# The second product by seven products in four chunks instead of two, with all attention ahead of them

## The chip, the cores and the metric

The kernel runs on one core of a Trainium2 chip. The metric is device time in microseconds, from the start of the execution to its end; three runs of the kernel before took 905.02, 905.95 and 906.45 us, the median is 905.95.

## The reference

There are two stages. The first is an attention over q, k, v of shape 8 batches x 8 heads x 576 positions x 64. It adds two outputs: a softmax attention among positions at most three apart, and a softmax attention on means of four positions, repeated four times. The second stage takes the result as x (4608 tokens x 512) through a feed-forward net:

```
h = x @ w_in                     # 512 -> 2048
g = h                  where h >= 1
    (h + 1)^2 / 4      where -1 < h < 1
    0                  where h <= -1
out = g @ w_out                  # 2048 -> 512
```

All is float32.

## The kernel before, in words

**Numbers.** A float32 operand of a big product is held as two parts in TensorE's fp32r type, a high part (a cast, on ACT) and a low part (the rest, a subtraction on DVE or POOL). A product is then three matmuls: high x high, low x high and high x low. Weights are cut into parts once, at the start (`convert`).

**Chunks.** The 4608 tokens go in nine chunks of 512. The hidden layer has 16 rows f of 128, taken in eight pairs j. Chunks 0 and 1 compute both products directly (`mm1`, L1083, and `second`, L1111: per row f and per tile t of 128 tokens three matmuls of 512 columns). From chunk 2 on the first product runs as seven products of half size (Winograd's form of Strassen's scheme, `winograd`, L1298): per pair j seven products of six matmuls, 256 columns each, with sums of weights (`sums_of_weights`, once) and of x (`sums_of_x`, per chunk), and sums of the products on DVE (L1308) and ACT (L1305).

**The second product by seven products.** From chunk `TWICE` = 7 on the second product does the same (`twice`, L1214): for each pair j seven products M1 to M7, each of six matmuls of 256 columns, which add up over j in seven PSUM banks (`SUMS`: 0, 1, 2, 4, 5, 6, 7). It needs the curve in three pieces (L1165 to L1167), sums S1 to S4 of the pieces (L1176), five pairs of parts (L1171, L1172), sums of w_out that `sums_of_second` has stored in DRAM (TA and TB, loaded again for each j), and at the end of a chunk seven sums of the banks (`outputs`, L1238). The last pair j of chunk 8 is done directly.

**Attention.** `attention(n)` handles one pair of heads; 32 pairs, four to a batch, are spread among the chunks, so that batch b is over when the first chunk that needs it begins. A pair takes on PE the scores (L399, L444), the transposes (L628, L653, L654) and the products with v (L706, L729); on DVE reductions, sums and normalizing (L381 to L571, L681, L786, L797); on ACT the exponentials; on POOL a subtraction (L508) and two sums of v over four positions, `half` and `quarter` (L580, L583). It writes x into a ring `xr` of 1024 tokens. Most of its tiles have one slot each (qk, v, vp, vd, sl, sp), and it uses PSUM banks 0 to 2.

**What sets the order.** Every operation is an `Op` of a `Plan` with its engine, a cost, the operations that it needs, and its buffers. Three tables hold the answer of a search that was made elsewhere: `ORDER` (the order of all operations), `OTHER` (which of them run on their second engine) and `PLACES` (the place of each buffer). `Plan.run` walks through `ORDER` with its costs, gives each operation a start, and sorts by it; `Plan.emit` writes out the instructions in that order, so each engine and SP's DMA queue have a fixed order. `emit` also lets an earlier matmul wait for a DMA that a later product needs, where the plan finds one with enough lead. `FILLS` puts filler matmuls (L256) into PE's idle time at the start. `sums_of_second` is created beside pairs `JOBS`, `JOBS` + 2 and so on, and the steps of the second products beside the first products of the next pair j, by the list at L1365 to L1374.

Of the kernel before, what the change touches and what calls it, by code (L numbers as in the profile page):

```python
# [8 lines left out]
F32 = mybir.dt.float32  # L9
# [20 lines left out]
RING = 2 * TOK  # L30
# [25 lines left out]
TWICE = B - 1  # L56
JOBS = 14
# [34 lines left out]
class Plan:  # L92


    LATENCY = 0.10
    PE_LATENCY = 0.25
    DMA_LATENCY = 2.0
    ISSUE = 0.45
    BACKLOG = 6.0
    AHEAD = 0.25  # L100
    LANDED = 1.2
    REACH = 2.5
    TO_PE = 0.04
    LATE = 0.10
    FREE = {"PE": 4.5, "ACT": 3.0, "DVE": 1.0, "POOL": 1.4, "SP": 0.75}
    SWITCH = {(0, 1): 0.09, (1, 0): 0.22, (0, 2): 0.02, (2, 0): 0.17, (1, 2): 0.05, (2, 1): 0.05}

# [21 lines left out]
    def run(self, order, other, places):  # L129

        free = dict(self.FREE)
        avail, busy, users, done = {}, set(), {}, set()
        dma_free = port_free = 0.0
        mode = 0
        last = None

        places = iter(places)

        def pick(b):
            units = b.places[next(places)]  # L140
            assert not any((b.pool, u) in busy for u in units)
            return max(avail.get((b.pool, u), 0.0) for u in units), units

        self.done = []
        for n in order:
            o = self.ops[n]
            e, cost, o.fn, port = o.ways[n in other][:4]
            o.eng = e
            assert n not in done and all(d.n in done for d in o.deps), o.name
            done.add(n)  # L150
            t = given = 0.0
            for d in o.deps:
                x = d.start if d in o.follows else d.end
                if d.eng != e:
                    x += self.PE_LATENCY if d.eng == "PE" else self.TO_PE if e == "PE" else self.LATENCY
                    given = max(given, x)
                t = max(t, x)
            t = max(t, free[e], port_free if port else 0.0, dma_free - self.BACKLOG if e == "SP" else 0.0)
            for b in o.bufs:
                if b.units is None:  # L160
                    x, b.units = pick(b)
                    busy.update((b.pool, u) for u in b.units)
                    x += self.TO_PE if e == "PE" else self.LATENCY
                    given, t = max(given, x), max(t, x)
            o.start = t
            if e == "SP":
                free[e] = t + self.ISSUE
                dma_free = max(dma_free, t + self.DMA_LATENCY) + cost
                o.end = dma_free
            else:  # L170
                if e == "PE":
                    if o.after[0] is last:
                        cost = o.after[1]
                    last = o
                    cost += self.SWITCH.get((mode, o.mode), 0.0)
                    if given > free[e] - self.AHEAD and (mode, o.mode) in ((0, 0), (0, 2)):
                        cost += self.LATE
                    mode = o.mode
                free[e] = t + cost
                o.end = t + cost + o.landing  # L180
                if o.moves:
                    dma_free = max(dma_free, t + self.DMA_LATENCY) + o.moves
                if port:
                    port_free = o.end
            self.done.append(o)
            for b in o.bufs:
                b.end = max(b.end, o.end)
                left = users[id(b)] = users.get(id(b), b.users) - 1
                if not left:
                    for u in b.units:  # L190
                        avail[b.pool, u] = b.end
                        busy.discard((b.pool, u))
        assert len(done) == len(self.ops)
        self.done.sort(key=lambda o: o.start)
        return max(o.end for o in self.done)

    def emit(self, tc, fills):
        at, seen, spare = {}, set(), []
        for i, o in enumerate(self.done):
# [5 lines left out]
            if o.eng == "PE":  # L205
                for d in o.deps:
                    if d.eng != "SP" or d.n in seen:
                        continue
                    seen.add(d.n)
                    for k, (j, ends, ins) in enumerate(spare):  # L210
                        if j > at[d.n][0] and ends > d.end + self.LANDED:
                            tc.add_manual_dep(ins, at[d.n][1].name, mybir.DependencyInfo(mybir.DependencyClass.Sync, mybir.DependencyReason.DATA))
                            del spare[k]
                            break
            made = o.fn()
            if o.eng == "SP":
                at[o.n] = i, made.ins
            elif o.eng == "PE":
                spare = [(i, o.end, x.ins) for x in reversed(made[1:])] if made else [x for x in spare if x[1] > o.end - self.REACH]


@with_exitstack
def attention_then_ffn(ctx: ExitStack, tc, qT, kT, vw, vp, vq, band, fours, w_in, w_out, out):
# [13 lines left out]
    minus = cpool.tile([P, P], F32, name="minus")  # L237
    nc.scalar.mul(minus, ident, -1.0)
# [85 lines left out]
    def attention(n):  # L324
# [155 lines left out]
        less = early and n in PE_MAX(K)  # L480
        if early:
            o_m = op("DVE", 0.815, lambda: nc.vector.tensor_reduce(mlb.tile, sl_n(), axis=AX.X, op=ALU.max),
                     [o_sl], [slp, mlb], kk[2], name=name + "max")
            if less:

                def less_max():
                    for c0, c1 in ((SL0, 512), (512, SL0 + NB * WIN)):
                        w0, w1 = (c0 - SL0) // WIN, (c1 - SL0) // WIN
                        nc.tensor.matmul(
                            sl_view()[:, c0 - SL0 : c1 - SL0],  # L490
                            minus,
                            mlb.tile[:, w0:w1].unsqueeze(2).broadcast_to([P, w1 - w0, WIN]),
                            start=False,
                            stop=True,
                            skip_group_check=True,
                        )

                o_s = op("PE", 1.16, less_max, [o_m], [slp, mlb], kk[2], name=name + "lm")
            else:
                o_s = op("DVE", 0.80, lambda: nc.vector.tensor_tensor(slf(), sl_n(), ml_n(), op=ALU.subtract),  # L500
                         [o_m, None if extra else before.get("x")], [slp, mlb, slb], kk[2], name=name + "sub")
        else:
# [7 lines left out]
        o_e = op("ACT", 0.74, lambda: nc.scalar.activation(slf(), sl_n() if less else slf(), AF.Exp, scale=0.125),  # L510
                 [o_s, None if extra else before.get("x")], [slb] + [slp] * less, kk[3], name=name + "exp")
# [65 lines left out]
        vdb = scratch("vd", [P if shares else KB, NKB, P], "vd")  # L577
# [4 lines left out]
        def quarter():  # L582
            nc.gpsimd.tensor_tensor(vdb.tile, vpb.tile[:, :, 0, :], vpb.tile[:, :, 1, :], op=ALU.add)  # L583
# [5 lines left out]
        def whole():  # L589
            nc.vector.tensor_reduce(vdb.tile, vpb.tile.rearrange("k n f c -> k n c f"), axis=AX.X, op=ALU.add)  # L590

        if by_pe:
# [15 lines left out]
            def vd_out(copy):  # L608
                copy(vdb.tile, vsp.tile[:KB, :, 0:P])
# [111 lines left out]
        def pp_quarters():  # L721

            for tail in range(2):
                for r, h in ((0, 0), (1, 1), (1, 0), (0, 1)):
# [4 lines left out]
                    nc.tensor.matmul(pp_v(r)[hs, cs] if tail else pp_v(r)[hs], vdb.tile[rs, tail, hs], w,  # L729
                                     start=not tail, stop=bool(tail), skip_group_check=True)  # L730

        def pp():
            for kb in range(NKB):
                for h in range(2):
# [3 lines left out]
                        vdb.tile[:, kb, hs],  # L738
# [5 lines left out]
        def pp_up():  # L744
            for kb in range(NKB):
                for i, c0, c1 in ((0, 0, QB), (1, 0, QB // 2), (1, QB // 2, QB), (2, 0, QB)):
                    for h in range(2):
# [3 lines left out]
                            vdb.tile[:, kb, h * D : (h + 1) * D],  # L751
# [647 lines left out]
def PE_MAX(k):  # L1399
    return range(k["pm1"])  # L1400


PLANNED = []
# [4 lines left out]
    pm1=0, pv1=2, pu1=1, o1=-7.22, o2=32.66, dk0=-0.05, tl3=20.0, tl=12.56, ts=10.88, so=60.0, sod=55.13, so2=-10.77,  # L1408
# [311 lines left out]
```

## Time and profile before

| what | value |
|---|---|
| median of three runs | 905.95 us (905.02 to 906.45) |
| profiled execution: first to last instruction | 904.0 us |
| around it (median less span) | 1.95 us |
| chunks 2 to 6, from one's first product to the next one's | 97 to 99 us |
| chunk 7, the same | 83 us |

The profile holds one execution. A row of the windows gives for each engine the time in which it was busy and its instructions in brackets. PE is the matmul engine, PEld its weight loads, which run beside the matmuls. Groups by line give the busy time, the mean of one instruction in ns, and the engine's idle time ahead of them with what ended it. L numbers are lines of the kernel before.

### The profile page before, as it was taken

The page shows a single profiled execution, that of the slowest core. Times are in us where ns is not written, and L with a number is a line of the kernel's source. Part 1 is how long each engine was busy: PE and PEld are TensorE (multiplying, and loading weights), DVE is VectorE, ACT ScalarE, POOL GpSimd, SP SyncE. Part 2 cuts the span into 40 slices and gives each one's busy share as a digit, 9 for nine tenths or more (in the row PEclk, how much of TensorE's full clock was granted, in tenths as well). Part 3 has the DMA queues.
Part 4 walks back from the last instruction along what each step waited for, and adds up shares of the span by engine and source line. Part 5 has one row for each costly group of instructions (what it writes and reads, how often), then busy time and mean ns, then how long its engine had stood idle before and what let it go on. Part 6 is the DMA issues. An engine that isn't in the chain of part 4 may idle for free.

```text
span 904.0 us, 21213 instructions
## 1 busy us (share of the span) xinstructions
PE 895.1 (99%) x8577; PEld 794.2 (88%) x8577; DVE 725.9 (80%) x1329; ACT 547.6 (61%) x1143; POOL 162.3 (18%) x154
## 2 busy tenths in 40 slices
PE   9899999999999999999999999999999999999998
PEld 8678888888898988898889888988898889999997
DVE  6999986888877787888878887888876777678767
ACT  5888865545565555656656556556655576576653
POOL 4544453232202100211211102120021000000000
PEclk9999999999999999999999999999999999999999
DMA  9984343676487657777687667776675468889982
GB/s 330 375 308 158 112 138 120 208 257 225 139 278 271 247 205 258 239 260 249 213 284 251 216 209 258 260 247 218 216 284 199 152 205 286 298 288 302 334 281 90
DMA packets 73226, 214.00 MB, mean 237 GB/s; under 512 B 8088, under 2 KB 11288, under 8 KB 73128
## 3 DMA queue, kind: packets, MB, share of 16 engines
q1 hardware_dynamic: 67864, 204.23, 65.6%
q10 hardware_dynamic: 5264, 8.42, 2.5%
q8 instruction: 67, 1.10, 0.5%
q14 instruction: 31, 0.25, 0.1%
HBM read 180.11 MB, written 32.51 MB: 235 GB/s over the span
## 4 chain that ended last, share of the span: by engine, by line
PE 96%; DVE 2%; ACT 1%; issue 0%; DVEq 0%; POOL 0%; POOLq 0%
PE ps L1111 34%; PE ps L1298 32%; PE ps L1083 9%; PE ps L1214 8%; PE ps L399 3%; PE ps L706 3%; PE ps L628 2%; PE ps L444 1%; PE ps L729 1%; PE ps L653 1%; PE ps L252 0%; DVE xr L1238 0%; PE ps L654 0%; PE ps L599 0%; DVE gt L1065 0%; DVE w_i L849 0%
## 5 line engine op out<-in xcount | busy, mean ns | idle before, releaser
L1111 PE MATMUL ps<-w_o,gt 128*128 128x512 f32 x1368 | 349.8, 395 | 0.6 <-DVE gt L1065 0.6
L1111 PEld LDWEIGHTS ps<-w_o,gt 128*128 128x128 f32 x1368 | 245.2, 188 | 47.4 <-DVE gt L1065 1.3
L1298 PE MATMUL ps<-T,lS 128*128 128x256 f32 x1008 | 147.7, 282 | 0.0
L1298 PEld LDWEIGHTS ps<-T,lS 128*128 128x128 f32 x1008 | 133.4, 188 | 3.9
L1305 ACT COPY tt<-ps 128x512 f32<-128x512 f32 x112 | 65.7, 586 | 94.5 <-PE ps L1298 93.8
L1308 DVE TENSOR_TENSOR tt<-ps,tt 128x512 f32<-128x512 f32 x112 | 62.4, 557 | 58.4 <-PE ps L1298 57.0
L1298 PE MATMUL ps<-B,lA 128*128 128x256 f32 x672 | 101.4, 286 | 0.0
L1298 PEld LDWEIGHTS ps<-B,lA 128*128 128x128 f32 x672 | 91.1, 188 | 7.6 <-ACT tt L1305 0.5
L1083 PE MATMUL ps<-x,w_i 128*128 128x512 f32 x384 | 95.7, 397 | 1.0 <-DVE x L875 0.4
L508 POOL TENSOR_TENSOR sl<-sl,mxl 128x640 f32<-128x640 f32 x29 | 39.9, 1374 | 291.9 <-DVE mxl L506 201.8
L1049 ACT ACTIVATE tt<-tt 128x512 f32<-128x512 f32 x82 | 51.5, 630 | 63.0 <-DVE tt L1308 53.3
L1063 ACT CAST gt<-tt 128x512 fp32r<-128x512 f32 x108 | 66.4, 621 | 37.5 <-PE ps L1111 21.8
L1083 PEld LDWEIGHTS ps<-x,w_i 128*128 128x128 f32 x384 | 70.8, 188 | 18.3 <-DVE x L875 0.9
L1065 DVE TENSOR_TENSOR gt<-tt,gt 128x512 fp32r<-128x512 f32 x96 | 70.3, 739 | 9.2 <-ACT gt L1063 8.6
L1054 ACT ACTIVATE tt<-tt 128x512 f32<-128x512 f32 x113 | 70.6, 630 | 2.3
L1061 DVE SCALAR_TENSOR_TENSOR tt<-tt 128x512 f32<-128x512 f32 x82 | 58.7, 722 | 9.1 <-ACT tt L1054 8.9
L580 POOL TENSOR_TENSOR vp<-vp 128x512 f32<-128x512 f32 (+1 forms) x30 | 41.7, 1391 | 87.4 <-DMA vp<-vq 85.0
L1308 DVE TENSOR_TENSOR tt<-tt 128x512 f32<-128x512 f32 x56 | 40.9, 731 | 13.4 <-ACT tt L1305 12.8
L1298 PE MATMUL ps<-B,lS 128*128 128x256 f32 x336 | 49.7, 284 | 0.0
L1298 PEld LDWEIGHTS ps<-B,lS 128*128 128x128 f32 x336 | 46.1, 189 | 3.4
L1298 PE MATMUL ps<-T,lA 128*128 128x256 f32 x336 | 49.0, 281 | 0.0
L1298 PEld LDWEIGHTS ps<-T,lA 128*128 128x128 f32 x336 | 43.9, 189 | 0.3
(155 smaller groups left out, 1471.9 us busy)
## 6 DMA issues: line engine op xcount, KB each, us to landing
lS<-S SPq DMA_DIRECT2D x112, 512.0 KB, 4.7
lA<-A SPq DMA_DIRECT2D x56, 512.0 KB, 5.0
vp<-vq SPq DMA_DIRECT2D x28, 512.0 KB, 5.1
lA<-A SPq DMA_DIRECT2D x56, 256.0 KB, 3.8
v<-vw SPq DMA_DIRECT2D x32, 320.0 KB, 4.5
raw_i<-w_in SPq DMA_DIRECT2D x16, 512.0 KB, 7.7
raw_o<-w_out SPq DMA_DIRECT2D x16, 512.0 KB, 8.4
qk<-qT SPq DMA_DIRECT2D x28, 288.0 KB, 3.8
```

The costliest lines, as they stand in the source:

```text
L580: nc.gpsimd.tensor_tensor(vpb.tile[:, :, 0:2, :], vpb.tile[:, :, 0:2, :], vpb.tile[:, :, 2:4, :], op=ALU.add)
L1049: o2 = op("ACT", 0.49 + e, lambda: nc.scalar.activation(u(), src(), AF.Relu, bias=0.5, scale=0.5), deps, [srcbuf, ub], key, name=f"relu {n ...
L1054: nc.scalar.activation(u(), u(), AF.Square)
L1061: o4 = op("DVE", v, lambda: nc.vector.scalar_tensor_tensor(g(), src(), 1.0, u(), op0=ALU.max, op1=ALU.min), [o3], [srcbuf, ub], key, name= ...
L1063: o5 = op("ACT", 0.50 + e, lambda: nc.scalar.copy(flat(gb.tile[:, 0]), g()), [o4], [held, gb], key, name=f"gh {name}")
L1065: engine.tensor_tensor(flat(gb.tile[:, 1]), g(), flat(gb.tile[:, 0]), op=ALU.subtract)
L1083: nc.tensor.matmul(hb.tile[:, 0, :], wb.tile[:, w, cc * P : (cc + 1) * P], xt[:, x], start=cc == 0 and i == 0, stop=cc == NCC - 1 and i == 2)
L1111: made = [nc.tensor.matmul(o, gb.tile[:, g, ts], wb.tile[:, w, :], start=i0 + i == 0, stop=i0 + i == 3 * nf - 1) for i, (g, w) in enumerat ...
L1214: made.append(nc.tensor.matmul(o, g.tile[:, gx, ts], w.tile[:, wx, ws], start=j == 0 and h == 0 and i == 0, stop=2 * j + 2 == last_f(c) an ...
L1298: made.append(nc.tensor.matmul(xy(dst), l(w, k), yb.tile[:, v, k], start=first and n == 0, stop=n == 5, skip_group_check=True))
L1305: return op("ACT", cost, lambda: nc.scalar.copy(to(), src()), deps, [tb, XY], kx[i], name=f"{name} {c},{j}")
L1308: return op("DVE", cost, lambda: nc.vector.tensor_tensor(to(), a(), b(), op=ALU.add), deps, held, kx[i], name=f"{name} {c},{j}", port=port)
```

## The change

`TWICE` goes from 7 to 5, so chunks 5 to 8 use the seven products for the second product too. The ring of x grows from two chunks to four, `JOBS` goes from 14 to 8, and a new `ORDER` has all attention over by the time the first of the second products of chunk 5 begins. For pairs from batch 1 on, the pooled v (`vd`) is no longer a tile of its own but the first part of vp's tile. An unused way to subtract the maximum on PE (`PE_MAX`, `less_max`) and its tile `minus` go. `Plan.run` with its costs becomes `Plan.place`, which only looks up places; the order of emission is now `ORDER` itself. Which earlier matmul waits for which DMA comes from a table `CARRIED`. `FILLS` goes from 39 matmuls to 27. The Bass object is made with a DMA scratch of 1024.

```diff
-RING = 2 * TOK
+NRING = 4
+RING = NRING * TOK
...
-TWICE = B - 1
-JOBS = 14
+TWICE = B - 3
+JOBS = 8
...
-    def run(self, order, other, places):
...
+    def place(self, order, other, places):
+
+        busy, users, done = set(), {}, set()
         places = iter(places)
...
+            o.eng, _, o.fn = o.ways[n in other][:3]
             assert n not in done and all(d.n in done for d in o.deps), o.name
             done.add(n)
...
+                    b.units = b.places[next(places)]
+                    units = {(b.pool, u) for u in b.units}
+                    assert not units & busy, o.name
+                    busy |= units
...
-    def emit(self, tc, fills):
...
+    def emit(self, tc, fills, carried):
...
             made = o.fn()
             if o.eng == "SP":
-                at[o.n] = i, made.ins
-            elif o.eng == "PE":
-                spare = [(i, o.end, x.ins) for x in reversed(made[1:])] if made else [x for x in spare if x[1] > o.end - self.REACH]
+                issued[o.n] = made.ins
+            for d, x in zip(carried.get(o.n, ()), reversed(made[1:] if made and o.n in carried else ())):
+                tc.add_manual_dep(x.ins, issued[d].name, mybir.DependencyInfo(mybir.DependencyClass.Sync, mybir.DependencyReason.DATA))
...
-    minus = cpool.tile([P, P], F32, name="minus")
-    nc.scalar.mul(minus, ident, -1.0)
...
-        vdb = scratch("vd", [P if shares else KB, NKB, P], "vd")
+        vdb = vpb if shares else sbuf("vd", [KB, NKB, P], F32, "w", SLOTS)
+
+        def vd():
+            return vpb.tile[:, :, 0, :] if shares else vdb.tile
...
         def quarter():
-            nc.gpsimd.tensor_tensor(vdb.tile, vpb.tile[:, :, 0, :], vpb.tile[:, :, 1, :], op=ALU.add)
+            nc.gpsimd.tensor_tensor(vd(), vpb.tile[:, :, 0, :], vpb.tile[:, :, 1, :], op=ALU.add)
...
-        places = [tuple(range(u, u + n)) for u in range(0, 8, n) if c == NCH or u // 4 == c % 2]
+        places = [tuple(range(u, u + n)) for u in range(0, 4 * NRING, n) if c == NCH or u // 4 == c % NRING]
...
-    total = plan.run(ORDER, OTHER, PLACES)
-    PLANNED.append((total, plan))
+    plan.place(ORDER, OTHER, PLACES)
     with tc.manual_schedule():
-        plan.emit(tc, FILLS)
+        plan.emit(tc, FILLS, CARRIED)
...
-FILLS = {17: (0, 9), 19: (5, 4), 97: (2, 21), 306: (3, 5)}
+CARRIED = {
+    334: (477,), 345: (501, 502), 362: (504,), 372: (528, 529), 385: (531,), 422: (555, 556), 435: (558,), 454: (770,
...
+FILLS = {17: (1, 3), 84: (1, 6), 101: (3, 11), 70: (6, 3), 306: (6, 4)}
...
-    nc = bacc.Bacc("TRN2", target_bir_lowering=False, num_devices=1)
+    nc = bacc.Bacc("TRN2", target_bir_lowering=False, num_devices=1, dynamic_dma_scratch_size=1024)
```

## Rows read from the trace of the kernel before

**Rows 1.** The page, parts 1 and 5: busy us, share, instructions.

```profile
PE 895.1 (99%) x8577; PEld 794.2 (88%) x8577; DVE 725.9 (80%) x1329; ACT 547.6 (61%) x1143; POOL 162.3 (18%) x154
...
L1298 PEld LDWEIGHTS ps<-T,lS 128*128 128x128 f32 x1008 | 133.4, 188 | 3.9
```

**Rows 2.** The page, part 4: the chain that ended last, by engine and line.

```profile
PE 96%; DVE 2%; ACT 1%; issue 0%; DVEq 0%; POOL 0%; POOLq 0%
PE ps L1111 34%; PE ps L1298 32%; PE ps L1083 9%; PE ps L1214 8%; PE ps L399 3%; PE ps L706 3%; PE ps L628 2%; PE ps L444 1%; PE ps L729 1%; PE ps L653 1%; PE ps L252 0%; DVE xr L1238 0%; PE ps L654 0%; PE ps L599 0%; DVE gt L1065 0%; DVE w_i L849 0%
```

**Rows 3.** Waits of PE and of DVE: us in total, times, longest us.

```profile
PE ps L252 <- POOL ident masks.py:199: 1.4, 1, 1.4
...
DVE tt L1308 <- PE ps L1298: 57.0, 81, 2.4
DVE tt L1061 <- ACT tt L1054: 23.3, 23, 5.5
```

**Rows 4.** Chain in time order and timeline: start us, us, instructions.

```profile
61.77 4.14 PE ps L1111 x18
154.12 2.81 PE ps L1111 x12
267.58 2.09 PE ps L1111 x9
...
853.80 0.87 PE L1214 MATMUL ps<-lTA,g 128*128 128x256 f32 x6
854.51 0.87 PE L1214 MATMUL ps<-w_o,g 128*128 128x256 f32 x6
855.22 0.88 PE L1298 MATMUL ps<-B,lA 128*128 128x256 f32 x6
```

**Rows 5.** Windows: length, busy us (instructions) by engine, PEclk, DMA share, GB/s.

```profile
0.00:35.00 35.00, 31.98 (x562) 27.51 (x562) 24.39 (x45) 22.05 (x55) 16.08 (x37) 1.00 0.96 354
35.00:140.00 105.00, 103.43 (x855) 82.59 (x852) 96.06 (x163) 82.67 (x166) 47.85 (x37) 1.00 0.53 188
140.00:728.00 588.00, 587.97 (x5795) 516.25 (x5794) 472.72 (x852) 338.04 (x702) 98.35 (x81) 1.00 0.67 231
728.00:893.00 165.00, 165.00 (x1343) 162.79 (x1342) 125.33 (x260) 103.17 (x219) 0.00 (x0) 1.00 0.81 273
40.00:60.00 20.00, 19.18 (x182) 14.78 (x183) 19.76 (x30) 16.79 (x35) 9.59 (x7) 1.00 0.84 319
60.00:100.00 40.00, 40.00 (x323) 32.41 (x322) 37.48 (x66) 34.82 (x71) 21.74 (x17) 1.00 0.48 165
```

**Rows 6.** DMA issues: count, KB each, median us to landing.

```profile
vp<-vq SPq DMA_DIRECT2D x28, 512.0 KB, 5.1
```

**Rows 7.** DVE by line and shape, 237 to 728 us: busy, mean ns, idle before.

```profile
L1065 DVE TENSOR_TENSOR gt<-tt,gt 128x512 fp32r<-128x512 f32 x79 | 57.0, 730 | 8.0 <-ACT gt L1063 7.5
L1061 DVE SCALAR_TENSOR_TENSOR tt<-tt 128x512 f32<-128x512 f32 x78 | 55.9, 724 | 9.1 <-ACT tt L1054 8.9
L1308 DVE TENSOR_TENSOR tt<-tt 128x512 f32<-128x512 f32 x40 | 29.9, 748 | 9.3 <-ACT tt L1305 8.8
L1308 DVE TENSOR_TENSOR tt<-ps,tt 128x512 f32<-128x512 f32 x40 | 27.6, 690 | 16.3 <-PE ps L1298 15.7
L1308 DVE TENSOR_TENSOR tt<-ps,tt 128x256 f32<-128x256 f32 x40 | 16.9, 423 | 19.1 <-PE ps L1298 18.4
L931 DVE TENSOR_TENSOR T<-tt,T 128x512 fp32r<-128x512 f32 x20 | 13.7, 684 | 0.3 <-ACT T L930 0.3
L931 DVE TENSOR_TENSOR B<-xr,B 128x512 fp32r<-128x512 f32 x15 | 11.5, 771 | 0.0
```

**Rows 8.** A line of DVE beside POOL, two of POOL, whole span.

```profile
L849 DVE TENSOR_TENSOR w_i<-tt,w_i 128x512 fp32r<-128x512 f32 x9 | 9.4, 1049 | 0.7 <-ACT w_i L844 0.7
L580 POOL TENSOR_TENSOR vp<-vp 128x512 f32<-128x512 f32 (+1 forms) x30 | 41.7, 1391 | 87.4 <-DMA vp<-vq 85.0
L583 POOL TENSOR_TENSOR vd<-vp 128x256 f32<-128x256 f32 (+1 forms) x30 | 25.4, 848 | 60.5 <-PE ps L729 59.6
```

More of the change, by code (lines that the diff above doesn't have):

```diff
@@ L92 @@
 class Plan:
[L95 to L106, printed above, removed]
     def __init__(self, warm=0.0, fill=None):
@@ L127, in op @@
         return o
-    def run(self, order, other, places):
[L131 to L135, printed above, removed]
+    def place(self, order, other, places):
+        busy, users, done = set(), {}, set()
         places = iter(places)
[L139 to L142, printed above, removed]
         self.done = []
@@ L146, in run @@
             o = self.ops[n]
-            e, cost, o.fn, port = o.ways[n in other][:4]
-            o.eng = e
+            o.eng, _, o.fn = o.ways[n in other][:3]
             assert n not in done and all(d.n in done for d in o.deps), o.name
             done.add(n)
[L151 to L157, printed above, removed]
@@ L158, in run @@
-            t = max(t, free[e], port_free if port else 0.0, dma_free - self.BACKLOG if e == "SP" else 0.0)
             for b in o.bufs:
                 if b.units is None:
[L161 to L184, printed above, removed]
@@ L185, in run @@
-            self.done.append(o)
+                    b.units = b.places[next(places)]
+                    units = {(b.pool, u) for u in b.units}
+                    assert not units & busy, o.name
+                    busy |= units
             for b in o.bufs:
-                b.end = max(b.end, o.end)
                 left = users[id(b)] = users.get(id(b), b.users) - 1
                 if not left:
-                    for u in b.units:
-                        avail[b.pool, u] = b.end
-                        busy.discard((b.pool, u))
+                    busy -= {(b.pool, u) for u in b.units}
@@ L193, in run @@
+            self.done.append(o)
         assert len(done) == len(self.ops)
-        self.done.sort(key=lambda o: o.start)
-        return max(o.end for o in self.done)
-    def emit(self, tc, fills):
-        at, seen, spare = {}, set(), []
-        for i, o in enumerate(self.done):
+    def emit(self, tc, fills, carried):
+        issued = {}
+        for o in self.done:
             if o.n in fills:
@@ L478, in ml_n @@
             return mlb.tile.unsqueeze(2).broadcast_to([P, NB, WIN])
-        less = early and n in PE_MAX(K)
         if early:
@@ L483, in attention @@
                      [o_sl], [slp, mlb], kk[2], name=name + "max")
[L484 to L501, printed above, removed]
+            o_s = op("DVE", 0.80, lambda: nc.vector.tensor_tensor(slf(), sl_n(), ml_n(), op=ALU.subtract),
+                     [o_m, None if extra else before.get("x")], [slp, mlb, slb], kk[2], name=name + "sub")
         else:
@@ L509, in attention @@
                      [o_m], [slb, mlb], kk[2], name=name + "sub", port=True)
-        o_e = op("ACT", 0.74, lambda: nc.scalar.activation(slf(), sl_n() if less else slf(), AF.Exp, scale=0.125),
-                 [o_s, None if extra else before.get("x")], [slb] + [slp] * less, kk[3], name=name + "exp")
+        o_e = op("ACT", 0.74, lambda: nc.scalar.activation(slf(), slf(), AF.Exp, scale=0.125),
+                 [o_s, None if extra else before.get("x")], [slb], kk[3], name=name + "exp")
         spb = scratch("sp", [P, NQB * SD + P * shares], "sp")
@@ L589, in whole @@
         def whole():
-            nc.vector.tensor_reduce(vdb.tile, vpb.tile.rearrange("k n f c -> k n c f"), axis=AX.X, op=ALU.add)
+            nc.vector.tensor_reduce(vd(), vpb.tile.rearrange("k n f c -> k n c f"), axis=AX.X, op=ALU.add)
         if by_pe:
@@ L608, in vd_out @@
             def vd_out(copy):
-                copy(vdb.tile, vsp.tile[:KB, :, 0:P])
+                copy(vd(), vsp.tile[:KB, :, 0:P])
             o_vs = op("PE", 1.2, fours_of, [l_v, l_fours, None if extra else before.get("x")], [vsp, vb, foursb], kk[4], name=name + "vs", mode=1)
@@ L728, in pp_quarters @@
                     w = apr()[rs, h].rearrange("k x s -> k (x s)")[:, r * QB // 2 : r * QB // 2 + SD // 2] if tail else apm()[rs, :, h, :]
-                    nc.tensor.matmul(pp_v(r)[hs, cs] if tail else pp_v(r)[hs], vdb.tile[rs, tail, hs], w,
+                    nc.tensor.matmul(pp_v(r)[hs, cs] if tail else pp_v(r)[hs], vd()[rs, tail, hs], w,
                                      start=not tail, stop=bool(tail), skip_group_check=True)
@@ L737, in pp @@
                         pp_v()[hs],
-                        vdb.tile[:, kb, hs],
+                        vd()[:, kb, hs],
                         apb.tile[:, kb, :, h, :],
```

18 lines of the change are left out of this document (3 added, 15 removed), and 541 rows, old and new, of tables (CARRIED, ORDER, OTHER, PLACES).

## The prediction, made before the changed kernel was run

> **What bounds the kernel now.** I read the page first: PE is busy 895.1 of 904.0 us, DVE 725.9 (80%) [rows 1], at a granted clock of 1.00 (the 2.4 GHz level) in every window [rows 5]; the chain that ended last is PE for 96%, and its longest lines are the three big products [rows 2]. The longest wait seen from PE is 1.4 us, at the start, while DVE itself waits 57 us for PE's first products [rows 3]. A busy PE could still be a slow one, so I asked for the pace next. In the chain, nine 128x512 matmuls take 2.09 us, twelve 2.80 and eighteen 4.14, so 230 to 234 ns, 232 taken; in the timeline of the last chunk, sets of six 128x256 matmuls begin at 853.80, 854.51 and 855.22, so 0.71 us for six, 118.3 ns each, whether they are the first product (L1298) or the second (L1214) [rows 4]. PE is therefore paced by its columns, back to back, from about 140 us to the last chunk. Last, the windows by stage: between 140 and 728 us PE is idle for 0.03 us, DVE is busy 472.7 of 588 us; between 728 and 893, where the second product already runs as seven products and no attention is left, PE is never idle [rows 5]. So time goes down with PE's columns, as long as DVE, the next engine, keeps up.
>
> The profiled execution has a span of 904.0 us, the median of the runs is 905.95: 1.95 us lie around the span. I take the change of the span and add it to the median.
>
> **The change part by part.**
>
> *Second product of chunks 5 and 6 (TWICE 7 to 5).* Removed: per chunk 16 rows f x 4 tiles x 3 = 192 matmuls of 512 columns at L1111, so 384; added: 8 pairs j x 42 = 336 of 256 columns at L1214, so 672. 384 x 232 ns = 89.1 us go, 672 x 118.3 ns = 79.5 us come: **-9.6 us** on PE. Ends: 384 x 230 - 672 x 119 = -8.4; 384 x 234 - 672 x 118 = -10.6. All of it lies on the path, since PE's work of each chunk follows the last without a gap.
>
> In one sentence by itself: the Trainium skill ("TensorE: Matmul & The Clock Gate", Back-to-back issue gap) gives a sustained spacing of about 131 ns for 512 columns and 81 for 128 when each matmul has its weight load; about 98 for 256 is my estimate between the two, and by it this step would cost 672 x 98 - 384 x 131, some 16 us more. Rows 4 contradict it for this data type: 232 and 118 ns, loads included.
>
> What the seven products add elsewhere: per pair j, DVE trades two 512-wide curves and two 512-wide low parts for three curves, five low parts and four sums. The two stages that have it already show the total: 125.3 us of DVE in 165 us, 76%, with PE full [rows 5]. ACT has 103.2 there, 63%. Hidden beside PE: 0. The extra loads (TA and TB, 512 KB each per j, as large as vp's, which land in 5.1 us [rows 6]) put the DMA share at 0.81 in that window against 0.67 before it; the same comes to chunks 5 and 6, cost 0. That chunks hand over well (T sums written into the earlier chunk's ring, outputs after it) is seen at the boundary 7 to 8, inside the same window.
>
> *All attention ahead.* Banks 0 to 2 and the slots sl, sp, v, vp, qk are needed by the seven products, so pairs 20 to 31 must be over where chunk 5 begins. No work is added, but its place changes: counted through the order table of the diff, the local products of the pairs of batches 2 to 7 stand 16 to 18 us of PE work apart, where they stand 21 to 24 apart now (with 30 and more at a chunk's turn). On PE this costs 0, as each pair takes its time in either place. On DVE it does cost. One feed-forward chunk of the present form takes on DVE, from the rows between 237 and 728 us (five chunks): 57.0 + 55.9 + 29.9 + 27.6 + 16.9 + 13.7 + 11.5, and 20 instructions of L913, of the same kind and size as L931's at 684 ns, 13.7, in all 226 / 5 = 45 us [rows 7]. Such durations overlap by their ends, so 45 is an upper figure; 41 is a lower one (I scale by the window's busy time over the sum of the groups' times, 0.91). Chunks 5 and 6 leave the stretch behind 140 us, and with them 82 to 90 of DVE's 472.7 us and 2 x 84.3 us of PE (per chunk 336 x 0.1183 + 192 x 0.232). What stays is 383 to 391 us of DVE beside 588 - 168.6 = 419 us of PE: **91 to 93%** against 80% now. Can DVE do that? Between 60 and 100 us it is 37.48 of 40 busy, 93.7%, with PE 40.00 full and POOL at 54%; between 40 and 60 it reaches 19.76 of 20, but there PE loses 0.8 us [rows 5]. So the demand sits at, or just under, the best share seen to cost nothing. With a sustained share s the stretch takes max(419, 387/s): no cost for s above 92.4%, 3 us at 91.7%, 11 us at 90%. Ends 0 and +13, taken **+1.0**: the nearest rows are those at 93.7%, but the order in which DVE takes its work is fixed, and somewhere in 400 us it will be late once or twice.
>
> Port: a DVE instruction with two SBUF inputs waits while POOL works; L849, run on DVE beside POOL, takes 1049 ns [rows 8] where L931, the same kind, takes 684 [rows 7]. POOL's work is the same per pair and no longer spread over 490 us but over 400. Some 0.3 us for each collision, and most of these are already in the durations above. Taken within the +1.0.
>
> *vd kept in vp's place.* The loaded tile now lives until the pair's products have read it, so the next pair's 512 KB load starts after them: 5.1 us to land [rows 6] and 1.4 + 0.85 us on POOL [rows 8], 7.4 us of the 16 to 18 us between pairs. Cover 9 us. The load is a wait on SP's queue, and the weight loads lA and lS stand behind it; the load of v, which needs the same products over, stands in that queue already, next to it, so nothing is held longer than now. Cost 0; if the cover goes, rival 3.
>
> *Ring of four chunks, scratch of 1024, no minus tile.* Space and one ACT instruction of 0.3 us at the start: 0. *Sums of the second weights from pair 8 instead of 14*: the same instructions, their DVE time is counted above as all of them lie in the stretch before and after; their stores and POOL neighbours keep their size.
>
> *Start.* Filler matmuls go from 39 to 27, DVE and POOL swap some conversions, and SP's order is new. The first 35 us hold 3.0 us of idle PE and move data at a DMA share of 0.96, and 35 to 140 another 1.6 us [rows 5]. Bytes don't change. Bounds: all of the 4.6 us goes, or as much comes again. Taken 0.
>
> *Carried waits.* Which earlier matmul waits for a DMA is now written in a table instead of found by a rule. A late DMA could cost PE something in either direction, but none of its longest waits is one [rows 3]; taken 0.
>
> Sum: 905.95 - 9.6 + 1.0 = **897.4**.
>
> **The rivals.**
> 1. *DVE becomes the bound (the other side).* Place: between 140 and about 560 us, above all chunks 2 to 4, where the order has a pair every 17 us. Price: 387/s - 419. It decides from a sustained share under 90.1%: then the time is 905.95 or more; at 89% it is 896.4 + 16 = 912. For it: this kernel holds 93.7% only for 40 us, its average is 80%, and the tail of a chain through ACT (L1061 waits on ACT for 23 us in all [rows 3]) needs room. Against: in that stretch DVE now waits mostly for PE (the 57 us of rows 3), that is, it is early, and such slack can be filled. In a milder form, s from 90.5 to 91.5%, the time is 900 to 904.
> 2. *The tables also take out the losses that are there.* The 4.6 us before 140 us go, and the 1.0 us that I took for DVE stays away: 896.4 - 4.6 = 891.8, so 891 to 894. For it: the start has idle PE. Against: its DMA share is 0.96.
> 3. *vp comes late.* If SP's queue holds the load more than 9 us behind other loads, each of 24 pairs makes PE wait 0.5 to 1 us: 897 + 12 to 24. Against: the share of DMA in that stretch is 0.67, and landings take 5 us.
> 4. *Matmuls priced by piece.* If the half-wide ones went at the pace of their loads (188 ns mean [rows 1]), the step would add 672 x 0.188 - 89.1 = 37 us. Rows 4 and 5 show the very same instructions at 118, so hardly any chance. (The skill's spacing, quoted above, is of this kind, and the trace does not bear it out.)
> 5. *It doesn't do what it says*: PE's columns don't fall, 905 to 907. The counts follow from the loops, so 0.01.
>
> **How the numbers follow.** Forecast (894 to 900) 0.62; rival 1 mild (900 to 904.1) 0.10, hard (over 904.1) 0.09; rival 2 0.12; rival 3 0.05; rivals 4 and 5 0.01 each. About 0.2%, 1.8 us, is what a measurement can tell from no change. Faster than 904.1: 0.62 + 0.10 + 0.12 = 0.84, lowered to 0.82 for causes I don't see. Within 0.2% (904.1 to 907.8): 0.01 of rival 5 and some 0.05 of rivals 1 and 3, 0.06. Slower: 0.12. The range 892.5 to 904.0 holds the forecast, the mild rival 1 and most of rival 2.
>
> **What would show it.** Right: 984 matmuls at L1111's successor and 1302 at that of L1214, at 232 and 118 ns; PE idle after 140 us under 2 us; chunk 5's first product at some 559 to 561 us and chunks 5, 6, 7 some 80 to 84 us apart; DVE at 91% or more before it and about 76 to 85% after. Rival 1: PE waits on DVE (sl, gt, xr) between 230 and 560 us, DVE at its own ceiling. Rival 2: PE idle under 2 us in the first 140. Rival 3: PE waits at the pair's products on POOL vp. I am wrong if chunk 5 starts after 568 us, or if the chunks behind it are over 85 us apart.

## The result, and the profile after

The changed kernel took 897.87 us (median of 4 runs, 895.42 to 899.19), the kernel before 905.49 on the same chip: ratio 0.9913, 95% interval 0.9896 to 0.9930. The forecast was 897.4, in a range of 892.5 to 904.0. Run again (run e1_same below) it took 899.71 against 905.97 (medians), ratio 0.9918 (0.9905 to 0.9931). The ratios are taken over all the runs, not from the two medians. The medians differ by 7.6 us where the sum has 8.6. That it came so near is partly luck: two of its terms were wrong by some 4 us each, with opposite signs.

The profiled execution (span 893.5 us) is the quickest of its four. The page's part 1, two lines of its part 4, and the groups of the two second products:

```profile
PE 886.2 (99%) x8853; PEld 798.6 (89%) x8853; DVE 761.6 (85%) x1464; ACT 563.6 (63%) x1217; POOL 162.1 (18%) x153
...
PE 94%; DVE 2%; DMA 2%; ACT 1%; issue 1%; POOL 0%; DVEq 0%; POOLq 0%; ACTq 0%; SPq 0%
...
L1030 PE MATMUL ps<-w_o,gt 128*128 128x512 f32 x984 | 255.5, 398 | 0.1
...
L1133 PE MATMUL ps<-lTA,g 128*128 128x256 f32 x372 | 54.4, 281 | 0.1
```

Against [rows 1] PE has 276 matmuls more (672 - 384 - 12 fillers) and is 8.9 us less busy; against [rows 2] DMA has come into the chain with 2% (landings of vp, of qk and of an output store), where it had no share. PE's and DVE's waits, as in [rows 3] (L1217, L980, L973 were L1298, L1061, L1054):

```profile
PE ps L185 <- POOL ident masks.py:199: 1.4, 1, 1.4
PE ps L625 <- ACT al L581: 0.6, 1, 0.6
```

```profile
DVE tt L1227 <- PE ps L1217: 33.9, 48, 1.6
DVE tt L980 <- ACT tt L973: 10.6, 14, 1.6
```

PE's longest wait is the same 1.4 us, and the others are short, so this execution by itself shows hardly a loss; DVE's slack against PE fell from 57.0 to 33.9 us. The pace, from the chain in order of time (start, us, instructions), is that of [rows 4]: nine matmuls of 512 columns in 2.10 us, six of 256 in 0.71, first product (L1217) and second (L1133) alike:

```profile
299.99 2.10 PE ps L1030 x9
302.08 0.70 PE ps L1217 x6
...
650.59 0.71 PE ps L1217 x6
651.30 0.71 PE ps L1133 x6
```

Windows by stage (columns as in [rows 5]), cut where chunk 0, chunk 1 and chunk 5 begin their first products; then the densest part of the third, and chunk 6 alone:

```profile
0.00:32.10 32.10, 29.75 (x551) 25.54 (x551) 24.80 (x45) 23.15 (x58) 18.61 (x37) 1.00 0.94 329
32.10:134.40 102.30, 102.30 (x893) 81.05 (x892) 91.76 (x158) 81.03 (x163) 41.96 (x36) 1.00 0.62 229
134.40:556.70 422.30, 421.25 (x4639) 363.53 (x4638) 379.75 (x710) 249.42 (x547) 101.57 (x81) 1.00 0.69 242
556.70:893.50 336.80, 332.88 (x2775) 328.54 (x2773) 265.25 (x554) 210.01 (x452) 0.00 (x0) 1.00 0.82 281
...
244.00:456.00 212.00, 211.90 (x2461) 187.16 (x2461) 196.40 (x367) 130.27 (x286) 46.75 (x37) 1.00 0.76 266
...
642.00:722.00 80.00, 80.00 (x675) 79.91 (x675) 65.64 (x138) 53.43 (x115) 0.00 (x0) 1.00 0.89 296
```

Three things are to be seen. The start is 3 us shorter (before, chunk 0 began at 35.1 us). Between 244 and 456 us DVE is 92.6% busy and PE still loses only 0.1 us. And chunk 6 takes 80 us, with 672 matmuls x 0.1183 = 79.5. The landings of vp, as in [rows 6], and of the stores of TA:

```profile
vp<-vq SPq DMA_DIRECT2D x28, 512.0 KB, 4.2
...
TA<-TAs SPq DMA_DIRECT2D x8, 512.0 KB, 3.5
```

### The profile page after: what moved, and what is told of

Read it like the earlier page. It is cut to its first block, busy times and chain, and to the rows that moved or that the text cites. A ratio compares the mean times of both kernels' runs of the same rounds, so it can differ in the third digit from the quotient of the medians.

```text
span 893.5 us, 22025 instructions
## 1 busy us (share of the span) xinstructions
PE 886.2 (99%) x8853; PEld 798.6 (89%) x8853; DVE 761.6 (85%) x1464; ACT 563.6 (63%) x1217; POOL 162.1 (18%) x153
## 4 chain that ended last, share of the span: by engine, by line
PE 94%; DVE 2%; DMA 2%; ACT 1%; issue 1%; POOL 0%; DVEq 0%; POOLq 0%; ACTq 0%; SPq 0%
PE ps L1217 31%; PE ps L1030 24%; PE ps L1133 16%; PE ps L1002 9%; PE ps L332 3%; PE ps L625 3%; PE ps L547 2%; PE ps L377 1%; PE ps L648 1%; PE ps L572 1%; DMA vp<-vq 1%; DMA qk<-qT 1%; DMA out<-tt 0%; PE ps L185 0%; PE ps L573 0%
## 5 line engine op out<-in xcount | busy, mean ns | idle before, releaser
L1030 PE MATMUL ps<-w_o,gt 128*128 128x512 f32 x984 | 255.5, 398 | 0.1
L1030 PEld LDWEIGHTS ps<-w_o,gt 128*128 128x128 f32 x984 | 175.4, 188 | 36.0 <-DVE gt L984 1.1
L1217 PE MATMUL ps<-T,lS 128*128 128x256 f32 x1008 | 147.7, 282 | 0.0
L1217 PEld LDWEIGHTS ps<-T,lS 128*128 128x128 f32 x1008 | 131.9, 189 | 2.1
L1224 ACT COPY tt<-ps 128x512 f32<-128x512 f32 x112 | 65.6, 586 | 59.1 <-PE ps L1217 58.5
L1217 PE MATMUL ps<-B,lA 128*128 128x256 f32 x672 | 101.9, 287 | 0.0
L1217 PEld LDWEIGHTS ps<-B,lA 128*128 128x128 f32 x672 | 88.9, 188 | 5.0 <-DVE tt L1227 0.5
L1227 DVE TENSOR_TENSOR tt<-ps,tt 128x512 f32<-128x512 f32 x112 | 62.2, 555 | 35.0 <-PE ps L1217 33.9
L1084 ACT ACTIVATE tt<-tt 128x256 f32<-128x256 f32 (+1 forms) x93 | 45.4, 489 | 58.2 <-DVE tt L1227 48.1
L457 ACT ACTIVATE sp<-ps,mxp 128x144 f32<-128x144 f32 x96 | 36.6, 381 | 35.9 <-DVE mxp L451 30.2
L1086 DVE SCALAR_TENSOR_TENSOR tt<-tt 128x256 f32<-128x256 f32 (+1 forms) x93 | 46.3, 509 | 10.1 <-ACT tt L1085 10.0
L1133 PE MATMUL ps<-lTA,g 128*128 128x256 f32 x372 | 54.4, 281 | 0.1
L1091 DVE TENSOR_TENSOR g<-s,g 128x256 fp32r<-128x256 f32 (+1 forms) x93 | 46.5, 508 | 8.9 <-ACT g L1090 8.5
L973 ACT ACTIVATE tt<-tt 128x512 f32<-128x512 f32 x80 | 50.6, 632 | 2.2 <-ACT tt L1046 0.4
L1090 ACT CAST g<-s 128x256 fp32r<-128x256 f32 (+1 forms) x93 | 42.6, 473 | 13.5 <-DVE s L1095 13.0
L968 ACT ACTIVATE tt<-tt 128x512 f32<-128x512 f32 x50 | 31.6, 632 | 30.8 <-DVE tt L1227 21.3
L984 DVE TENSOR_TENSOR gt<-tt,gt 128x512 fp32r<-128x512 f32 x64 | 48.6, 762 | 1.7 <-ACT gt L982 1.4
```

The lines of the kernel that those rows point to most:

```text
L973: nc.scalar.activation(u(), u(), AF.Square)
L984: engine.tensor_tensor(flat(gb.tile[:, 1]), g(), flat(gb.tile[:, 0]), op=ALU.subtract)
L1030: made = [nc.tensor.matmul(o, gb.tile[:, g, ts], wb.tile[:, w, :], start=i0 + i == 0, stop=i0 + i == 3 * nf - 1) for i, (g, w) in enumerat ...
L1084: o2 = op("ACT", a, lambda: nc.scalar.activation(u(), src(), AF.Relu, bias=0.5, scale=0.5), deps, [hb, ub], kk[k], name=f"relu {c},{j},{wh ...
L1086: return op("DVE", v, lambda: nc.vector.scalar_tensor_tensor(src(), src(), 1.0, u(), op0=ALU.max, op1=ALU.min), [o3], [hb, ub], kk[k], nam ...
L1091: o2 = op("DVE", v, lambda: nc.vector.tensor_tensor(dst()[:, 1], src(), dst()[:, 0], op=ALU.subtract), [o1], [srcbuf, buf], kk[k], name=f" ...
```

## The experiments

Ratios are to the kernel before, on the same chip, with 95% intervals; two runs are compared by the difference of their ratios, times 906 us. The dense stretch is the one from chunk 1's first product to that of the first chunk that has no pair of attention of its own (chunk 5; in the kernel before and in e6 and e8 chunk 7). Line numbers of a run may be a few higher than the changed kernel's.

**e1_same: the changed kernel again.**

> The changed kernel again, unaltered, for a narrower interval and a second profile. Both theories: 896 to 899 us, ratio to the kernel before 0.990 to 0.993. If DVE is at its limit in the stretch from 134 to 557 us, that stretch differs by 1 to 3 us from the first profile and PE waits on DVE there; if the executions differ by something else, the difference lies at the start or is spread.

0.9918 (0.9905 to 0.9931), 897.11 to 899.97 us. Its profiled execution, 898.0 us, is 4.5 us longer than the first one, and shows what that one lacks. Its windows, the same two stages:

```profile
134.70:560.60 425.90, 421.93 (x4639) 364.07 (x4638) 381.32 (x710) 249.29 (x547) 101.27 (x81) 1.00 0.69 240
560.60:898.00 337.40, 333.44 (x2775) 328.59 (x2773) 265.49 (x554) 209.49 (x452) 0.00 (x0) 1.00 0.80 280
```

PE is idle 4.0 us in the dense stretch against 1.05 in the first profile, with the same work. The longest wait, in the chain of waits:

```profile
265.20 9.69 DMA TA<-TAs
274.92 0.35 ACT TBs L945
...
275.44 0.59 ACT tt L1224
276.08 0.98 PE ps L1217 x6
```

Read it backwards: PE's product waits for a copy out of its bank (L1224), the copy stands on ACT behind a cast (L945), and the cast waits until TA, whose staging tile it writes, has been stored. The store took 9.69 us; a 512 KB store of TA takes 3.5 us in the median of the first profile. PE's next waits in that stretch are 1.0 us on DVE (L980, behind a load of qk that took 5.93 us) and 0.7 us on ACT; the first profile has the wait on DVE too, with 0.5 us.

**e2_undo_both and e11_undo_one: the second product direct again** in chunks 5 and 6 (e2) or 5 alone (e11), with all attention still ahead.

```
-TWICE = B - 3
+TWICE = B - 1        # e11: B - 2
-            if c > TWICE:        # sums of x keep their ring places
+            if c > B - 3:
...                               # ORDER: direct steps in the places of the others
```

> Chunks 5 and 6 get the direct second product back, 384 matmuls of 512 columns in place of 672 of 256; attention, its order, the ring, the tables of the rest stay as in the changed kernel. Theory (the gain is PE's columns, 9.6 us): 897.9 + 9.6 = 907.5, between 906 and 909.5, so 1 to 3 us slower than the kernel before. Rival (the gain came from the new tables or the start): under 902.

> As e2, but chunk 5 alone gets its direct second product back (192 matmuls of 512 columns in place of 336 of 256). Columns: 4.8 us. In e2 another 12 us came from waits at places where the direct form meets an order made for the other one. Theory: 4.8 us and 2 to 7 of such waits, 7 to 12 us slower than the changed kernel, with the difference less the waits at 4.8. Rival (columns are no price there): the difference less the waits at 2 or under.

e2: 1.0152 (1.0129 to 1.0175); e11: 1.0102 (1.0088 to 1.0116). So undoing costs 21 and 17 us beside e1's ratio, not 9.6 and 4.8; both are outside what was expected. Chunks 5 to 7 of e2, of e1 and one stretch of e2, windows:

```profile
564.00:831.00 267.00, 258.67 (x1779) 234.15 (x1777) 146.30 (x269) 142.03 (x268) 0.00 (x0) 0.99 0.60 204
...
680.00:700.00 20.00, 16.72 (x94) 14.48 (x93) 7.39 (x12) 8.04 (x14) 0.00 (x0) 0.91 0.40 142
```

```profile
561.00:806.00 245.00, 244.89 (x2061) 241.90 (x2060) 194.60 (x408) 158.19 (x342) 0.00 (x0) 1.00 0.83 288
```

Of the 22 us, PE's idle time is 8.3 - 0.1 = 8.2; the busy time grew by 13.8, which holds the 9.6 us of columns, some 1.8 us of a lower granted clock (an estimate: the 0.91 over 20 us above) and 2.4 us more that are not explained. In e11, read in the same way, PE is idle 7.8 us and busy 8.3 us longer, where the columns are 4.8. Two waits of e2, us in total, times, longest:

```profile
PE ps L1217 <- ACT tt L1224: 4.7, 3, 3.3
PE ps L1030 <- ACT tt L1046: 1.4, 2, 1.1
```

A direct chunk without attention beside it doesn't run full in this order: DVE is at 55%, and nothing fills PE while a copy (L1224, L1046) is late. So the columns' worth can't be read from the undoing. In this order, which was made for the other form, attention ahead with the old second product is a loss of 1.5%; what an order made for it would give, no run shows.

**e10_pe_more and e7_pe_less: 96 matmuls of 256 columns more, or fewer**, in the second product of chunks 5 and 6 (48 each, 11.4 us in all; e10 repeats the low x high part of M3 to M5, the low part of the curve's factor with the high part of the weights', and e7 leaves it out).

```
-for i, (gx, wx) in enumerate(((0, 0), (0, 1), (1, 0))):
+kinds = ((0, 0), (0, 1), (1, 0))[: 2 if c < 7 and x in ("M3", "M4", "M5") else 3]   # e7
+kinds = ((0, 0), (0, 1), (1, 0)) + ((1, 0),) * (c < 7 and x in ("M3", "M4", "M5"))  # e10
+for i, (gx, wx) in enumerate(kinds):
```

> The changed kernel with the third matmul of M3, M4 and M5 made twice in chunks 5 and 6: 96 matmuls of 256 columns more, 11.4 us at 118.3 ns (the low part of one factor counts twice there). e7 took 96 away and gained 1 to 2 us, as PE then waits on the copies out of the first product's bank. Theory (PE's columns and the loop through that bank are about equally long, so what is added costs in full and what is removed gains nothing): 10 to 12.5 us slower than the changed kernel. Rival (the loop alone sets the pace of chunks 5 and 6): under 5 us slower.

> The changed kernel without one of the three matmuls of M3, M4 and M5 in chunks 5 and 6 (96 of 256 columns left out). Theory (PE's columns bound chunks 5 and 6 at 118.3 ns each): 11.4 us less than the changed kernel, between 10 and 12. Rival (DVE or loads bound these chunks): less than 7 us.

e10: 1.0044 (1.0029 to 1.0059), 0.0126 above e1, 11.4 us, as its theory said: the columns count in full. In its profile chunks 5 to 7 take 88.9, 85.1 and 82.0 us, 10.0 more than e1's 85.5, 80.2 and 80.3, and PE is never idle in chunk 6:

```profile
650.00:735.00 85.00, 85.00 (x722) 85.00 (x721) 65.64 (x138) 53.51 (x115) 0.00 (x0) 1.00 0.82 280
```

e7: 0.9903 (0.9891 to 0.9916), 0.0015 below e1, 1.4 us of 11.4, within the intervals; what was expected of it failed. Chunk 6 of e7, and the waits of PE's weight loads there and in chunk 5, two of e7 and then the only one of e1 on that line:

```profile
645.00:724.00 79.00, 77.65 (x624) 74.61 (x624) 65.48 (x138) 53.01 (x114) 0.00 (x0) 1.00 0.86 298
```

```profile
PEld ps L1218 <- DVE tt L1228: 3.2, 13, 0.3
PEld ps L1218 <- ACT tt L1225: 2.9, 6, 1.1
...
PEld ps L1217 <- ACT tt L1224: 0.2, 1, 0.2
```

The chunk has 5.7 us less to do and is 1.0 us shorter (79.2 against e1's 80.2). The first product has one bank left (3; `SUMS` takes the seven others); it can't start its next product before ACT and DVE have copied the last one out. The waits that appear in e7 are for these copies, so with the second product a little shorter, that round (product, copy, product) sets the pace.

**e6_before_start: the kernel before with the changed tables up to the middle of chunk 0**, fillers included, the old order behind.

```
-ORDER, OTHER, PLACES, FILLS                # before
+the changed kernel's up to `m1 0,8`, then the old order of what is left
```

> The kernel before with the changed kernel's start alone: its order, engines, places and fillers for all that stands ahead of row 8 of chunk 0 (some 75 us), the order of before behind it. Theory (the new tables save 3 us of idle PE at the start, which my sum had at 0): first product of chunk 0 at 32 us instead of 35, the whole 2.5 to 4 us faster than the kernel before. Rival (what the start saves is lost in chunk 0 to the conversion of weights): within 1 us of the kernel before.

0.9959 (0.9946 to 0.9972): 3.7 us come from the start alone. Its start, window:

```profile
0.00:32.10 32.10, 29.76 (x551) 25.67 (x551) 25.05 (x45) 23.30 (x59) 17.44 (x34) 1.00 0.95 337
```

PE's idle time there fell from 3.0 to 2.3 us [rows 5], its busy time from 32.0 to 29.8. The 12 fillers that are gone are 256 columns each, 1.4 us at 118.3 ns, so they are at most half of the 3.0 us by which the start is shorter; e6 takes over order, engines, places and fillers together, and no run separates them.

**e3_dve_more, e8_before_dve_more, e4_dve_less: DVE's load.** The sum of k is made twice for pairs 8 to 31 in the changed kernel (e3) and in the kernel before (e8); e4 leaves out the normalizing of those pairs' local attention (and so computes something else).

```
+def kd_sum(n=n):                                    # e3, e8
+    for _ in range(2 if n >= 8 else 1):
+        nc.vector.tensor_reduce(kdb.tile, ...)
...
-o_n = op("DVE", 0.82, lambda: nc.vector.tensor_tensor(
+o_n = op("DVE", 0.82, lambda: n < 8 and nc.vector.tensor_tensor(   # e4
```

> In the changed kernel the sum over k of pairs 8 to 31 is made twice, 24 x 0.74 = 17.8 us more DVE, nearly all between 134 and 557 us, where DVE is busy 380 of 423 us. Theory (PE bounds it, DVE has its last room there): +0 to +4 us, DVE at 94% in that stretch. Rival (DVE is the bound of the stretch already): +14 to +18 us, PE idle or late by as much.

> The kernel before with the same addition as in e3, the sum over k made twice for pairs 8 to 31, 17.8 us more DVE. There it lies between 140 and 728 us, where DVE is busy 80%. Theory (what e3 cost is the room that the change has used up): 0 to 3 us slower than the kernel before, where e3 cost 12. Rival (a DVE instruction at that place delays the pair's chain whatever the load): 9 us slower or more.

> The changed kernel without the normalising of the local attention for pairs 8 to 31, 24 x 0.82 = 19.6 us less DVE. Theory (DVE is covered): 0 to -1.5 us, the same stalls of about 0.1 us left on PE. Rival (DVE costs time in the dense stretch): -5 us or more.

e3: 1.0066 (1.0052 to 1.0081), 13.4 us above e1. That is just under the rival's 14 to 18 us and far over the theory's 4. e8: 1.0012 (1.0004 to 1.0021), 1.1 us, as its theory said. e4: 0.9939 (0.9916 to 0.9963), no gain. The dense stretch of the three, in this order:

```profile
134.00:573.00 439.00, 428.44 (x4642) 363.96 (x4641) 400.69 (x734) 249.33 (x547) 103.47 (x81) 1.00 0.67 233
```

```profile
141.00:733.00 592.00, 590.09 (x5799) 516.79 (x5798) 491.76 (x878) 338.90 (x703) 99.36 (x81) 1.00 0.67 230
```

```profile
134.00:558.00 424.00, 421.41 (x4641) 364.04 (x4640) 367.77 (x688) 249.52 (x544) 102.06 (x81) 1.00 0.69 241
```

About 19 us more of DVE (400.69 - 381.32) lengthen the stretch by 13, about 14 us less don't shorten it. DVE's load is therefore not what the changed kernel waits for, but DVE has little room left before it is: some 6 us, the difference of 19 and 13 (an estimate). e3's waits of PE there name DVE, as rival 1 said they would:

```profile
PE ps L335 <- DVE xr L719: 2.6, 4, 0.8
PE ps L1033 <- DVE gt L987: 2.3, 5, 0.8
PE ps L1220 <- DVE tt L1230: 2.0, 5, 0.7
```

**e5_tb_apart, e9_tb_later, e12_ta_apart: taking e1's wait at 275 us away.** e5 stages TB in a slot of its own, e12 stages TA in one, e9 moves the steps for TB some 5 us of PE's work later.

```
+apart = {0: 24, 1: 24, 2: 22, 3: 35, 5: 20, 6: 18}.get(j)      # e12: {0: 30, 1: 24, 3: 35, 6: 18}
+tsb = fb if apart is None else sbuf("ts", [P, 2, 512], F32R, "w", [apart])
+sb = fb if x == "TA" else tsb                                   # e12: tsb if x == "TA" else fb
...
 TBh 0, TBl 0, sTB 0 later in ORDER; oa2 1 just ahead of oa1 1    # e9
```

> In the changed kernel TB's parts are staged in a free weight slot of their own for six of the eight pairs j, so ACT's cast of TB no longer waits for the store of TA to land (in the second profile that store took 9.7 us, the cast stood behind it on ACT, a copy behind the cast, and PE lost 1.8 us). Theory (part of the gain is lost to landings that hold ACT or DVE in the dense stretch, this one the largest): 1 to 2.5 us faster than the changed kernel, ratio to the kernel before 0.989 to 0.9905, and no wait of PE that goes back to TA's store. Rival (one of many small delays, another takes its place): the changed kernel's ratio of 0.9915 to within 0.0007.

> The changed kernel with one place of its order altered: the steps that stage and store TB of the first pair j stand some 5 us of PE work later, and the first sum of the next pair j 8 us later, so ACT reaches the cast of TB after the store of TA has landed even when that takes 10 us. Theory (this one store, in a stretch where DMA is at 0.86, costs 1.6 to 1.8 us in most executions): 1 to 2 us faster than the changed kernel, ratio to the kernel before 0.9893 to 0.9905, no wait of PE near 274 us. Rival (another landing takes its place, as in e5): ratio 0.9913 or more.

> The changed kernel, its order untouched, with TA's parts (not TB's) staged apart for four pairs j, in weight slots that no store has used for at least 11 us of PE work and that nothing takes for 15 us behind; TB stays where it was. So the cast of TB waits for no store, and no new wait on a young store comes in, as it did in e5 and e9. Theory (that one landing costs 1.6 to 1.8 us in most executions): 1 to 2 us faster than the changed kernel, ratio to the kernel before 0.9893 to 0.9908, no wait near 274 us. Rival (the stretch is tight as a whole, another landing shows at once): ratio 0.991 or more, with a new wait of PE over 1 us between 244 and 350 us.

e5: 0.9996 (0.9983 to 1.0008); e9: 0.9970 (0.9955 to 0.9985); e12: 0.9941 (0.9923 to 0.9958). None gained: beside e1's ratio e5 is 7.1 us slower and e9 4.7, beyond the intervals, and e12 2.1 us, where the intervals overlap. In each the old wait was gone and another stood there. The chain of e5, of e9 and of e12:

```profile
268.77 8.82 DMA S<-S34s
...
277.61 0.35 ACT ts L952
...
278.14 0.59 ACT tt L1231
```

```profile
281.43 7.55 DMA qk<-kT
289.00 0.75 DVE kd L319
...
293.88 0.70 DVE gt L984
294.62 0.79 PE ps L1030
```

```profile
266.88 9.98 DMA lA<-A
...
277.00 0.47 PE ps L1037
```

In e5 the new slot had a store to wait for itself; in e9 a load that landed after 7.55 us held DVE's queue; in e12 PE waited for a weight load of 256 KB that took 9.98 us. This stretch moves data at a high share, in the kernel before as well; between 265 and 275 us, before and e12:

```profile
265.00:275.00 10.00, 10.00 (x106) 8.92 (x99) 6.90 (x15) 5.21 (x13) 3.25 (x3) 1.00 0.93 312
```

```profile
265.00:275.00 10.00, 10.00 (x67) 8.99 (x66) 9.60 (x17) 7.75 (x18) 3.71 (x3) 1.00 0.91 294
```

The DMA share is nearly the same, but DVE has 9.6 of 10 us of work where it had 6.9, and ACT 7.8 where it had 5.2. The reading that suggests itself is that a landing that comes 4 us late fitted into the slack of these queues before and doesn't now. It is argued and not shown: no run took the DMA load away, and in e12 it was PE itself that waited for its load.

## Why the prediction came out right

**Columns, -9.6: right.** Counts (984; 372 shown of 1302 second products by seven, the rest in groups of other weights) and paces came as forecast, chunk 6 took 80 us where the sum has 79.5, and e10 charged 11.4 us for 11.4 us of the same matmuls. What the step didn't see is how near the limit lies: 11.4 us of columns further on, the first product's round through its bank gives back only 1.4 (e7).

**Start, 0 taken: wrong by 3.7 us.** e6 gives -3.7 (-2.5 to -4.9 by its interval), inside the step's bounds. The step looked at PE's idle time alone: of the 3.0 us by which the start became shorter only 0.7 were idle time and 2.3 busy time, of which the fillers are 1.4. Nor did the DMA share of 0.96, rival 2's counterargument, stand against it: the shorter start has 0.95. Rival 2 had this half of the case.

**What comes back, +1.0 taken, for the dense stretch: about +5.5, and not all of it there.** From the ratios the change is worth 7.4 (0.9918) to 7.9 us (0.9913) of some 906; the start's 3.7 and the columns' 9.6 would make 13.3, so 5.4 to 5.9 have come back (7.0 by the medians of e1). The profiles agree in sum. PE's busy and idle time over the whole span:

| kernel | PE busy | PE idle | span |
|---|---|---|---|
| before | 895.1 | 8.9 | 904.0 |
| e6 (new start only) | 892.1 | 8.9 | 901.0 |
| after | 886.2 | 7.3 | 893.5 |
| e1 (after, again) | 887.3 | 10.7 | 898.0 |

From e6 to e1 the columns should take 9.6 and the span fell by 3.0: 1.8 came back as idle time and 4.8 as busy time, though the work is the same; from e6 to the first profile it is -1.6 and 3.7. Where it came back can be read from e6's windows for the dense stretch (there from chunk 1 to chunk 7) and for what follows:

```profile
136.60:726.60 590.00, 588.88 (x5798) 516.76 (x5797) 475.74 (x854) 338.01 (x703) 98.47 (x81) 1.00 0.66 230
726.60:901.00 174.40, 170.06 (x1369) 166.47 (x1367) 131.86 (x269) 104.97 (x220) 0.00 (x0) 1.00 0.76 261
```

By the sum 590.0 - 168.6 = 421.4 us of the dense stretch should stay: the first profile has 422.3, e1 425.9, so +0.9 and +4.5. Behind it 174.4 + 159.0 = 333.4 were due (two more chunks of 79.5), and 336.8 and 337.4 came, +3.4 and +4.0; about 2 us of this are attention's last matmuls, which run to 566 us (an estimate from their paces), in sum work that moved from chunk 0, which is 2.2 and 1.8 us shorter than e6's 104.5. So in the quicker execution the dense stretch cost what the step had taken for it, in the other one 3.5 us more, and chunks 5 to 8, which the sum had at 0, cost 1 to 2 us in both: chunks 6 and 7 take 79.9 to 80.4 us each instead of 79.5.

Of the idle time, e1's longest wait is traced above. The busy part (matmuls that take longer without a visible wait) isn't explained by any run. DVE's demand was sized a little high: 379.75 of 422.3 us, 89.9%, where 91 to 93 was forecast. The step asked what share DVE can sustain, and took its +1.0 for DVE being late once or twice. e4 shows that less DVE work returns nothing, so the loss isn't DVE's load; the longest wait traced goes through ACT, behind a late landing. That landings are the cause of the whole, or of the difference between executions (895.4 to 900.0 us here), is not shown.

**vd in vp's place, 0: right.** No wait of PE names vp, and vp lands in 4.2 us (median), 5.1 before; the first profile's chain does pass through one landing of vp, at 172 us, but PE is idle for only 0.08 us behind it. **Loads of TA and TB, 0: right in chunks 5 to 7** (PE idle 0.1 us of 245), but their making was not free: the stores of TA stand in the chain at 265 us of e1. **Port: within the term.** The Trainium skill ("GPSIMD Engine Reference", 1. Specifications) says that VectorE shares its SBUF interfaces with GpSimd where its instruction has two SBUF inputs; the mean of gt (L1065 before, L984 now, two such inputs) over the whole execution went from 739 ns to 762, 64 x 23 ns = 1.5 us of DVE, and by e4 so little DVE work is nothing in the time. Carried waits, the ring and the scratch, also put at 0, were not tested by themselves.

**The rivals.** 1: not reached, but near: with the added load of e3 DVE sustains 91.3% (400.69 of 439 us), inside the 90.1 to 92.4% on which the step turned (by its own formula 905.95 us is reached at 90.3%, not 90.1%), and by that formula the changed kernel's 380 us then still fit (380 / 0.913 = 416, under 419). 2: its start came; its dense stretch came in the quicker execution and not in the other. 3, 4 and 5: no.

**The signs.** Chunk 5 began at 556.7 and 560.6 us (559 to 561 said); chunks 5, 6 and 7 stand 85.2, 79.9 and 80.4 us apart (80 to 84 said; the first holds the last products of attention, which end at 566 us). So the first is just over the 85 us that the prediction gave as a sign of being wrong; that limit left out the attention behind chunk 5's start. DVE's share before chunk 5 is 89.9%, under the 91% said. "PE idle under 2 us after 140 us" was badly put: the kernel's end alone had 4.3 us before (175.1 us with 170.8 of PE); in the dense stretch it was 1.05 us in the first profile and 4.0 in e1.

## What to carry to other kernels

Price matmuls by their columns at the pace in the trace, and then ask what loop (product, copy out, next product through one bank) is next: here one more cut of 11.4 us gave 1.4. When the room of a start is bounded, count its fillers with the idle time: they are busy time that can go (here 1.4 us, beside 0.7 of idle time). When an engine goes from 80 to 90%, ask not only whether its work fits, but which queues are held by a landing and how late that landing may come.

## What the runs showed of the hardware

Some landings take 1.8 to 3 times their median: 8.82 us (e5's store of S34, 512 KB, median 5.0), 9.69 us (e1's store of TA, 512 KB, median 3.2) and 9.98 us (e12's load of lA, 256 KB, median 3.8). Two of the three came at DMA shares of 0.95 (e1) and 0.91 (e12, both between 265 and 275 us), the third at 0.69 (e5, 260 to 280 us). The Trainium skill ("DMA: Bandwidth & Descriptors", Latency and other measured facts) gives 2 us of HBM access at high load against 0.2 in the mean; what the three add to their medians, 4 to 6.5 us, is more than that. They are counted from the issue, so they hold the wait behind other transfers too.

The second thing is the granted clock after a short stop of PE. In e12, where PE waited 1.7 us up to 277 us, the ten microseconds from 275 on had a mean granted clock of 0.83, between the levels of 2.4 GHz (1.00) and 1.2 GHz (0.5). That is some 1.7 us lost (0.17 of 10 us, an estimate), as much as the wait itself. In e1, after a wait of 1.6 us at the same place, the clock stayed at 1.00. So a wait can cost twice its length, and need not. The windows of e12 and of e1:

```profile
275.00:285.00 10.00, 8.30 (x136) 6.92 (x135) 6.62 (x14) 4.10 (x8) 0.57 (x1) 0.83 0.69 246
...
275.00:285.00 10.00, 8.92 (x147) 7.72 (x148) 8.34 (x16) 6.19 (x12) 1.16 (x1) 1.00 0.68 254
```
